# Attention fed into two mixture layers on one core: pv of the first token half one slot later, the second pair of head groups one slot later, and the q, k, v and p loads issued on SP

## The chip, the core and the metric

The kernel runs on one core of a Trainium2 chip. It is measured in device microseconds for one execution of the whole program. The engines named below are PE (TensorE: matmuls, with PEld for its weight loads), ACT (ScalarE), DVE (VectorE), POOL (GpSimd) and SP (SyncE, which here only issues DMAs). Each engine runs its own instructions in the order in which the program wrote them, and waits on semaphores for the others.

## What is computed

Cut to what matters, with 4 batches, 8 heads, 576 tokens of 64 values, 32 packed queries per head, and random float32 inputs:

```python
def sm_attn(qq, kk, vv):
    s = scale * np.matmul(qq, kk.transpose(0, 1, 3, 2))
    a = softmax(s)                     # max taken off, sum plus 1e-9
    return np.matmul(a, vv)
p_packed = sm_attn(p, k, v)            # 32 rows per head
out = sm_attn(q, p_packed, p_packed)   # 576 rows per head
x = out laid out as (2304, 512)
for e in range(4):                     # first mixture, weights by domain_probs
    y += prob[:, e:e+1] * (relu(x @ w1[e]) @ w2[e])
logits = y @ phi                       # second mixture: 8 experts, 4 slots each
d, c = softmax over tokens, softmax over slots
slot_out = expert MLP (m1, m2) of d.T @ y
result = c @ slot_out                  # (2304, 512)
```

## The kernel before, in words

A head part (about 70 us) loads weights, folds w2 and phi into one matrix, and computes the attention of batch 0. Then the main loop (`for sl in range(nslot + 1)`, L878) runs 128 slots: 32 per batch. A slot computes 2 x 6 matmuls of the first mixture (`mm1`, L477, "step M") for one expert and one block of 128 hidden features, for the batch whose attention is ready. Every fourth slot (0, 4, 8, ... of a batch) it first folds the next weights with the packed attention values (`make_g`, L447, "step G": 16 matmuls into two PSUM buffers, then two ACT casts L458 and two DVE subtractions L459, the second of which reads PSUM last) and adds logits (L504, "step L"). Beside it the attention of the next batch is computed piecewise by two generators, one for heads 0 to 3 (called g0 here) and one for heads 4 to 7 (g1). Each is resumed once per slot, in step A, and runs to its next `yield`. Within a slot the steps are written in the order F, G, L, M, S, A, P: F is the flip of the slot before (DVE L487, POOL L488), S the softmax of the batch before, P pours hidden activations of the batch before into sums (`pool_slots`, L648, in slots 4, 5 and 6 of a batch, for the batches after the first; its DVE reads are L666 to L672).

So the order on each engine is fixed by the slot in which a piece is written. In this text slot 20 is the 21st slot of a batch, G20 the step G in it, M20 its twelve matmuls and M20_1 the second six of these.

g0 starts in slot 0, g1 in slot OFF1, which is 9. A generator of a later batch does, slot by slot from its start: flip of p and of the first half of k (DVE L309, L292); flip of the second half of k and the scores `sa` (PE L301); `sa` again; maximum; exponential; scaling and transpose into `et` (DVE L332, L334); four ACT copies of the first token half of `et` into `etm` (L340); pv of the first half (36 small matmuls, L350); four copies of the second half into the same `etm`; pv of the second half with an ACT copy of the result to `gl` (L361); then the second attention with q (scores `sb`, exponential L394, and so on) until ACT casts the attention result into `a2` (L413) and POOL subtracts (L414), nine slots after the second pv.

Two resources matter below. `etm` is one buffer in the main loop, so the copies of the second half wait for pv of the first. And M, G, pv and the scores take their PSUM buffers from one ring of four (`mm_ps`), in turn; while a pv sum stands, its buffer is skipped and the others turn through three:

```python
def mm_ps(name, keep=None):
    i = (turns["mm"] + 1) % 4
    while i in kept.values():
        i = (i + 1) % 4
```

The loads of the next heads are queued as each buffer comes free (`feed`): the first half of k for the next group after pv of the first half, the second half of k after pv of the second, q after the flips of k, v after the flips of q. They are issued at the start of the slot behind (`run_due`), before by POOL. The 1 MB loads of w1 (L169) and, towards the end, the stream of the second mixture's weights (L749) are issued by SP.

Of the kernel before, what the change touches and what calls it, by code (L numbers as in the profile page):

```python
# [18 lines left out]
def tile_packed_attention_moe_softmoe(  # L19
# [15 lines left out]
    pe, act, dve, pool, sp = nc.tensor, nc.scalar, nc.vector, nc.gpsimd, nc.sync  # L35
# [20 lines left out]
    PLACE = ((0, 1, 2, 3), (4, 1, 2, 3)) * 2  # L56
    PIECES = ((0, 6), (6, 12), (12, 18))
    ENDS = ((0, 4), (4, 8), (8, 12), (12, 16), (16, 18))
    OFF1 = 9
    HEAD = "000101001011w1001w0011w10w0w1100w10w0101w1w1Gwww10w1G10w"  # L60
    LOADS = "PKkvaqVbQcXd1Wn2W3"
    WARM = 16
# [33 lines left out]
# [4 lines that stand above are left out]
        turns["mm"] = i  # L100
        if keep is not None:
            kept[keep] = i
        return ps_mm[i].tile([128, 512], F32, tag="mm", name=name)
# [25 lines left out]
    def a_tile(tag, name, bufs=1):  # L129
        return att_pool.tile([128, S], F32, tag=tag, name=name, bufs=bufs)  # L130
# [2 lines left out]

    def load_p(b, g, eng=None):
        t = att_pool.tile([128, D], F32, tag="p", name=f"p{b}{g}", bufs=2)
        (eng or pool).dma_start(t, p[b, 4 * g : 4 * g + 4].rearrange("h m d -> (h m) d"))
        qkv_t["p", b, g] = t

    def load_half(src, nm, b, g, hf, t=None, eng=None):
        if t is None:  # L140
            t = a_tile("qkv", f"{nm}{b}{g}{hf}", 4)
        t = t.rearrange("p (x d) -> p x d", d=D)
        (eng or pool).dma_start(
            t,
            src[b, 4 * g : 4 * g + 4].rearrange("h (t x) d -> (h t) x d", x=NBLK)[
                :, HB * hf : HB * hf + HB, :
            ],
        )
        qkv_t[nm, b, g, hf] = t
# [132 lines left out]
    def attention(b, g, feeds, ptb, pkb, etb, tmp, gp):  # L282
# [3 lines left out]
        def feed(key):  # L286
            if key in feeds:
                due.append(feeds[key])
# [48 lines left out]
        for hf in range(2):  # L337
            for h in range(4):
                r = slice(32 * h, 32 * h + 32)
                act.copy(  # L340
                    etb[hf % len(etb)][r, h % 2, :, 32 * (h // 2) : 32 * (h // 2) + 32],
                    et[r, HB * hf : HB * hf + HB, :],
                )
            yield
            vn = qkv_t.pop(("v", b, g, hf))
            if pv is None:
                pv = mm_ps(f"pv{bg}", bg)
            for x in range(HB):
                for par in range(2):
                    pe.matmul(  # L350
                        pv[64 * par : 64 * par + 64, :64],
                        vn[:, x, :],
                        etb[hf % len(etb)][:, par, x, :],
                        start=(hf == 0 and x == 0),
                        stop=(hf == 1 and x == HB - 1),
                        tile_position=(0, 64 * par),
                    )
            feed(f"k{hf}")
            if hf == 0:
                yield  # L360
# [59 lines left out]
    def start_attention(b, g):  # L420
        feeds = {}
        nb, ng = (b, 1) if g == 0 else (b + 1, 0)

        def later(src, nm, hf, bb, gg):
            return lambda: load_half(src, nm, bb, gg, hf)

        for hf in range(2):
            feeds[f"q{hf}"] = later(q, "q", hf, b, g)
            if nb < NB:
                feeds[f"k{hf}"] = later(k, "k", hf, nb, ng)  # L430
                feeds[f"v{hf}"] = later(v, "v", hf, nb, ng)
        if nb < NB:
            f = feeds["k0"]
            feeds["k0"] = lambda: (load_p(nb, ng), f())
        return attention(b, g, feeds, pt, pkt[:, g], [etm], att_tmp, pool)
# [335 lines left out]
    with tc.manual_schedule():  # L771
# [5 lines left out]
        def load_pair(src, nm, b, g, ts=None):  # L777
            for hf in range(2):
                load_half(src, nm, b, g, hf, ts and ts[hf], eng=sp)

        def load_next():
            load_pair(k, "k", 1, 0)
            load_p(1, 0, sp)
            load_pair(v, "v", 1, 0)

        loads = {
            "P": lambda: (load_p(0, 0, sp), load_p(0, 1, sp)),
            "K": lambda: load_pair(k, "k", 0, 0),
            "k": lambda: load_pair(k, "k", 0, 1, [hd0[:, 0], hd0[:, 1]]),
# [40 lines left out]
        def head_tmp(tag, name):  # L830
            if tag == "kt":
                return ht_pool.tile([128, S], F32, tag="ht", name=name)
            return spare[tag]

        gens = {
            "0": attention(0, 0, {}, pt, pkt[:, 0], [etm, et_x[0]], att_tmp, dve),
            "1": attention(
                0, 1, {}, pp1, pkt[:, 1], [et1, et_x[1]], head_tmp,
                pool if GP1 == "pool" else dve,
# [38 lines left out]
        for sl in range(nslot + 1):  # L878
# [3 lines left out]
            b, i = divmod(n, NU)  # L882
# [6 lines left out]
            if run and b + 1 < NB:  # L889
                if sl % 32 == 0:  # L890
                    att_gens.append(start_attention(b + 1, 0))
                if sl % 32 == OFF1:
                    att_gens.append(start_attention(b + 1, 1))
            def step_attention():
                for gen in list(att_gens):
                    if next(gen, "end") == "end":
                        att_gens.remove(gen)
                        if b + 2 == NB and not att_gens and sl % 32 > OFF1:
                            att.close()
# [94 lines left out]
        for i in range(2):  # L994
# [9 lines left out]
            for k, t in enumerate((ps, ps2)):  # L1004
                t = t.rearrange("p (j l r q) -> p r j l q", j=2, l=2, r=2)
# [127 lines left out]
        for so, (d0, dw) in zip(sos, PARTS):  # L1133
            project(1, CHUNK // dw, dw, [(so, 0, dw)])
            h = slice(d0, d0 + dw)
# [9 lines left out]
            for x0 in range(0, NBLK, nt):  # L1145
                ob = out_tile()
                for x in range(x0, x0 + nt, nb):
                    m = min(nb, x0 + nt - x)
# [41 lines left out]
```

## Time and profile before

| | |
|---|---|
| median of 3 runs | 534.63 us (533.45 to 535.47) |
| the profiled execution | 533.26 us, of which 531.5 us are the span of the core |
| PE busy | 492.4 us, 93% of the span |
| DVE, ACT, POOL busy | 55%, 44%, 47% |
| granted TensorE clock, mean | 0.984 of full speed |

The span has three stretches. The head goes to about 70 us. The main loop runs from there to about 428 us with PE nearly without a gap. After it the last sums are poured, and from about 450 us to the end the weights of the second mixture stream in with the DMA engines full. Times in the rows below are in us from the start of the span. In a row of the timeline the first number is the start, the second the duration (of all the instructions merged in the row), and the brackets tell how long the engine had stood idle before it and what ended that.

### The profile page before, as it was taken

What the parts mean: (1) busy time and instruction counts of PE and PEld (TensorE: products, weight loads), DVE (VectorE), ACT (ScalarE), POOL (GpSimd) and SP (SyncE); (2) the same over time, 40 slices, a digit from 0 to 9 for tenths busy, and PEclk for the clock granted to TensorE, in tenths of its full rate; (3) what the DMA queues carried; (4) which work ended last, traced back from release to release, by engine and by line L of the source; (5) the groups of instructions that cost most, each with busy time, mean ns of one, the idle gap of its engine ahead of it and who ended that gap; (6) DMA issues with size and microseconds to landing.
All of it is one profiled execution on the core that took longest, in us unless ns stands there. A gap on an engine that the chain in (4) does not pass through costs nothing.

```text
span 531.5 us, 12898 instructions
## 1 busy us (share of the span) xinstructions
PE 492.4 (93%) x5404; PEld 347.1 (65%) x5404; DVE 293.1 (55%) x539; ACT 235.6 (44%) x539; POOL 247.9 (47%) x310
## 2 busy tenths in 40 slices
PE   7897999999999999999998999999999987998883
PEld 5775787777865777787557778775778864224232
DVE  6265555756667666568775655676554544311031
ACT  3857555565552447465324564651345421111031
POOL 8512446597652467975326566852446531200000
PEclk9999999999999999999999999999999998998997
DMA  8999145343430353443204424351368459999998
GB/s 280 367 373 312 47 151 190 113 151 102 158 126 1 116 182 105 151 155 115 90 2 149 152 93 141 121 209 71 120 224 332 159 192 367 409 408 408 374 326 288
DMA packets 66713, 104.06 MB, mean 196 GB/s; under 512 B 4368, under 2 KB 50192, under 8 KB 66656
## 3 DMA queue, kind: packets, MB, share of 16 engines
q1 hardware_dynamic: 62640, 93.10, 49.6%
q0 software_dynamic: 3232, 9.75, 6.2%
q8 instruction: 42, 0.69, 0.6%
q10 hardware_dynamic: 784, 0.39, 0.3%
q14 instruction: 15, 0.12, 0.1%
HBM read 98.52 MB, written 4.72 MB: 194 GB/s over the span
## 4 chain that ended last, share of the span: by engine, by line
PE 65%; DMA 13%; ACT 8%; DVE 8%; issue 3%; POOL 3%; SPq 0%; POOLq 0%; DVEq 0%; ACTq 0%
PE h L477 32%; PE sl L648 7%; DMA ck<-in_moe_w_dram 7%; PE lg L504 6%; PE g L447 5%; DMA hn<-in_moe_w_dram 3%; ACT etm L340 3%; PE sa L301 3%; PE pv L350 3%; PE sb L301 3%; DMA k<-in_k_dram 2%; PE o L1151 1%; PE w2t L255 1%; POOL hn L488 1%; PE pw L241 1%
## 5 line engine op out<-in xcount | busy, mean ns | idle before, releaser
L477 PE MATMUL h<-a,g 128*128 128x288 f32 x1536 | 226.1, 302 | 2.5 <-POOL a L414 1.6
L477 PEld LDWEIGHTS h<-a,g 128*128 128x128 f32 x1536 | 208.0, 188 | 28.3 <-issue 22.3
L488 POOL TENSOR_TENSOR hn<-hn,dp_sb 128x576 f32<-128x576 f32 x128 | 151.4, 1188 | 123.2 <-DVE hn L487 118.9
L481 ACT ACTIVATE ht<-h 128x288 f32<-128x288 f32 x256 | 103.6, 411 | 149.3 <-PE h L477 149.0
L487 DVE STREAM_TRANSPOSE hn<-ht 128x576 f32<-128x576 f32 x128 | 96.6, 761 | 55.0 <-ACT ht L481 54.9
L459 DVE TENSOR_TENSOR g<-g,g 128x512 fp32r<-128x512 f32 x64 | 41.2, 685 | 26.6 <-ACT g L458 26.6
L648 PE MATMUL sl<-hn,dpt 32*32 32x512 f32 x1152 | 48.2, 597 | 1.5 <-DVE dpt L607 1.2
L458 ACT CAST g<-g 128x512 fp32r<-128x512 f32 x64 | 34.3, 588 | 21.1 <-PE g L447 21.0
L504 PE MATMUL lg<-ht,wphi 128*32 128x288 f32 x512 | 37.8, 412 | 0.0
L447 PE MATMUL g<-w,gl 64*32 64x512 f32 x512 | 35.7, 601 | 0.2 <-DVE tacc L666 0.2
L648 PEld LDWEIGHTS sl<-hn,dpt 32*32 32x32 f32 x1152 | 21.0, 103 | 21.4 <-issue 11.0
L504 PEld LDWEIGHTS lg<-ht,wphi 128*32 128x32 f32 x512 | 13.5, 109 | 32.7 <-issue 25.5
L350 PE MATMUL pv<-etm,v 128*64 128x64 f32 x468 | 19.0, 225 | 6.6 <-ACT etm L340 3.5
L414 POOL TENSOR_TENSOR a<-a,a 64x576 fp32r<-64x576 f32 x14 | 19.9, 1424 | 9.6 <-ACT a L413 8.9
L350 PEld LDWEIGHTS pv<-etm,v 128*64 128x64 f32 x468 | 16.2, 138 | 10.7 <-ACT etm L340 5.7
L340 ACT COPY etm<-et 32x288 f32<-32x288 f32 x52 | 22.3, 428 | 1.7 <-DVE et L334 0.5
L382 DVE STREAM_TRANSPOSE nat<-sb 128x288 f32<-128x288 f32 x14 | 6.8, 483 | 25.5 <-PE sb L301 25.5
L1120 PE MATMUL so<-hn,tacc 128*32 128x384 f32 (+1 forms) x104 | 18.2, 492 | 2.6 <-DMA hn<-in_moe_w_dram 2.6
L666 DVE TENSOR_TENSOR tacc<-sl,tacc 128x512 f32<-128x512 f32 (+2 forms) x32 | 15.3, 546 | 9.4 <-PE sl L648 9.4
L260 ACT COPY hn<-w2t 128x512 f32<-128x512 f32 x32 | 17.1, 588 | 6.0 <-PE w2t L255 6.0
L255 PE MATMUL w2t<-ident,hn 128*128 128x128 f32 x128 | 17.4, 279 | 2.2 <-ACT hn L260 2.2
L301 PE MATMUL sa<-k,pt 128*128 128x288 f32 x56 | 16.7, 425 | 1.9 <-DVE k L292 1.4
(179 smaller groups left out, 484.8 us busy)
## 6 DMA issues: line engine op xcount, KB each, us to landing
w<-in_moe_w_dram SPq DMA_DIRECT2D x32, 1024.0 KB, 5.4
hn<-in_moe_w_dram SPq DMA_DIRECT2D x42, 512.0 KB, 9.5
ck<-in_moe_w_dram SPq DMA_DIRECT2D x42, 512.0 KB, 9.1
hn<-in_moe_w_dram SPq DMA_DIRECT2D x14, 384.0 KB, 8.5
q<-in_q_dram POOLq DMA_DIRECT2D x12, 288.0 KB, 3.3
k<-in_k_dram POOLq DMA_DIRECT2D x10, 288.0 KB, 3.3
v<-in_v_dram POOLq DMA_DIRECT2D x10, 288.0 KB, 3.3
out_dram<-ob SPq DMA_DIRECT2D x7, 384.0 KB, 5.2
```

What stands on the lines that cost most here:

```text
L301: pe.matmul(ps[:, :HS], lhs[:, j, :], t[:, :, j, :], start=(j == 0), stop=(j == 1))
L340: act.copy(etb[hf % len(etb)][r, h % 2, :, 32 * (h // 2) : 32 * (h // 2) + 32], et[r, HB * hf : HB * hf + HB, :],)
L350: pe.matmul(pv[64 * par : 64 * par + 64, :64], vn[:, x, :], etb[hf % len(etb)][:, par, x, :], start=(hf == 0 and x == 0), stop=(hf == 1 an ...
L447: pe.matmul(pss[g][32 * ((c + 2 * g) % 4) : 32 * ((c + 2 * g) % 4) + 32, :], gl[b % 2][r, c, :], t[r, c], start=True, stop=True, tile_posi ...
L458: act.copy(hi, pss[g])
L459: dve.tensor_tensor(out=lo, in0=pss[g], in1=hi.bitcast(F32), op=ALU.subtract)
L477: pe.matmul(ps[:, :HS], gg[:, l, g, e % 2, fs], r[:, ts], start=(g == 0 and t == 0), stop=(g == 1 and t == 2),)
L481: act.activation(out=ht[:, ts], in_=ps[:, :HS], func=AF.Relu)
L487: dve.transpose(out=own, in_=unturned.pop((n, kf, e)).rearrange("p (x t) -> p x t", t=32))
L488: pool.tensor_tensor(out=own, in0=own, in1=dp_sb[:, n // NU, :, e].unsqueeze(2).to_broadcast([128, NBLK, 32]), op=ALU.mult,)
L504: pe.matmul(lg_t[b, pr][32 * c : 32 * c + 32, :HS], wphi[:, 2 * i + kf, 32 * e : 32 * e + 32], ht_t[n, kf, e][:, HS * hf : HS * hf + HS], ...
L648: pe.matmul(pss[f][c : c + 32, :], dpt[r, x, :], hn[r, p0 : p0 + NU, x, 2 * ep : 2 * ep + 2].rearrange("p n e k f -> p n (e k f)"), start= ...
```

## The change

Three edits. The first load line of each helper takes SP instead of POOL as its default engine: this concerns the 37 loads of q, k, v and p in the main loop, since those of the head name SP already. `OFF1` goes from 9 to 10, so g1 starts a slot later. And for batches after the first an extra `yield` stands between the four copies of the first half into `etm` and pv of that half. All that follows in a generator comes a slot later; with the later start, g1 is two slots later from its first pv on. (The printed line numbers of the changed kernel are two higher from L345 on.)

```diff
-    OFF1 = 9
+    OFF1 = 10
...
     def load_p(b, g, eng=None):
...
-        (eng or pool).dma_start(t, p[b, 4 * g : 4 * g + 4].rearrange("h m d -> (h m) d"))
+        (eng or sp).dma_start(t, p[b, 4 * g : 4 * g + 4].rearrange("h m d -> (h m) d"))
...
     def load_half(src, nm, b, g, hf, t=None, eng=None):
...
-        (eng or pool).dma_start(
+        (eng or sp).dma_start(
...
             yield
+            if b and not hf:
+                yield
             vn = qkv_t.pop(("v", b, g, hf))
```

Three places show how this moves the instructions. In the names, h2_0_2_1 is the second token half (last digit) of the first mixture for block 2 and expert 2 (first and third digit); g3_0 the folded weights of block 3; a2_10 and a2_11 the attention result of the next batch; pv3, et3 belong to g1 of batch 1, pv4 to g0 of batch 2. A wait in brackets names the engine waited for.

ACT around slots 18 to 20 of the first batch of the loop, before:

```order
L413 CAST a2_10_1469<-a22_1444 64x576 [waits DVE_49]
L413 CAST a2_11_1470<-a22_1444 64x576
L361 COPY gl1_114<-pv3_1400 128x64 [waits PE_49]
L481 ACTIVATE ht2_1_1_1498<-h2_1_1_0_1499 128x288 [waits PE_49]
L481 ACTIVATE ht2_1_1_1498<-h2_1_1_1_1507 128x288 [waits PE_49]
L458 CAST g3_0_1529<-g3_0_0_1530 128x512 [waits PE_49]
L458 CAST g3_0_1529<-g3_0_1_1531 128x512 [waits PE_49]
```

The same place after the change:

```order
L483 ACTIVATE ht2_1_1_1467<-h2_1_1_0_1468 128x288 [waits PE_49,Activation_49]
L483 ACTIVATE ht2_1_1_1467<-h2_1_1_1_1476 128x288 [waits PE_49]
L415 CAST a2_10_1484<-a22_1440 64x576 [waits DVE_49]
L415 CAST a2_11_1485<-a22_1440 64x576
L340 COPY etm_117<-et3_1347 32x9x32 [waits Activation_49] x4
L460 CAST g3_0_1496<-g3_0_0_1497 128x512 [waits PE_49]
L460 CAST g3_0_1496<-g3_0_1_1498 128x512 [waits PE_49]
```

The two casts into `a2` and the four copies of the second half now stand between the last relu of slot 19 and the casts of G20; before, the relus of slot 19 stood there alone.

PE in slot 20 of the same batch, before:

```order
L477 MATMUL h2_0_2_0_1553<-a2_00_660,g2_1_1356 128x288 x3
L477 MATMUL h2_0_2_0_1553<-a2_01_661,g2_1_1356 128x288 x3
L477 MATMUL h2_0_2_1_1561<-a2_00_660,g2_1_1356 128x288 x3
L477 MATMUL h2_0_2_1_1561<-a2_01_661,g2_1_1356 128x288 x3
L477 MATMUL h2_0_3_0_1578<-a2_00_660,g2_1_1356 128x288 [waits DVE_49]
```

And after:

```order
L479 MATMUL h2_0_2_0_1520<-a2_00_660,g2_1_1351 128x288 x3
L479 MATMUL h2_0_2_0_1520<-a2_01_661,g2_1_1351 128x288 x3
L479 MATMUL h2_0_2_1_1528<-a2_00_660,g2_1_1351 128x288 [waits DVE_49]
L479 MATMUL h2_0_2_1_1528<-a2_00_660,g2_1_1351 128x288 x2
L479 MATMUL h2_0_2_1_1528<-a2_01_661,g2_1_1351 128x288 x3
L352 MATMUL pv3_1442<-etm_117,v111_1268 64x64 [waits DMAHW3_49,Activation_49]
```

M20_1 had no wait and now has one on DVE; pv of the second half, which stood in slot 18, follows it.

PE at slots 7 and 8 of the second batch of the loop, before:

```order
L477 MATMUL h4_1_3_1_2286<-a2_11_1470,g4_1_1859 128x288 x3
L350 MATMUL pv4_2294<-etm_117,v200_1525 64x64 [waits DMASW4_49,DVE_49,Activation_49]
L350 MATMUL pv4_2294<-etm_117,v200_1525 64x64 [waits Activation_49]
L350 MATMUL pv4_2294<-etm_117,v200_1525 64x64 x16
L447 MATMUL g5_1_0_2320<-w1_5_1_1910,gl1_114 32x512 [waits DMAHW7_49,DVE_49]
L447 MATMUL g5_1_1_2321<-w1_5_1_1910,gl1_114 32x512 [waits Activation_49]
```

And after:

```order
L479 MATMUL h4_1_3_0_2278<-a2_11_1485,g4_1_1859 128x288 x3
L479 MATMUL h4_1_3_1_2286<-a2_10_1484,g4_1_1859 128x288 [waits Activation_49]
L479 MATMUL h4_1_3_1_2286<-a2_10_1484,g4_1_1859 128x288 x2
L479 MATMUL h4_1_3_1_2286<-a2_11_1485,g4_1_1859 128x288 x3
L449 MATMUL g5_1_0_2297<-w1_5_1_1910,gl1_114 32x512 [waits DMAHW5_49,DVE_49]
L449 MATMUL g5_1_1_2298<-w1_5_1_1910,gl1_114 32x512 [waits DVE_49]
```

With pv gone from between them, G8 follows M7 at once, and both of its buffers now wait for DVE, not one.

## Rows read from the trace of the kernel before

**Rows 1.** Windows: start:end, length, busy (x count) by engine, PEclk, DMA share, GB/s

```profile
70.00:95.00 25.00, 23.81 (x245) 18.84 (x245) 15.07 (x25) 13.04 (x32) 14.46 (x23) 1.00 0.49 159
...
376.00:428.00 52.00, 52.00 (x475) 42.22 (x476) 27.43 (x38) 25.09 (x58) 29.22 (x25) 1.00 0.59 213
...
434.00:444.00 10.00, 9.34 (x288) 5.79 (x256) 1.41 (x4) 0.00 (x0) 0.46 (x2) 1.00 0.63 218
...
464.00:474.00 10.00, 10.00 (x73) 2.84 (x72) 2.06 (x4) 1.59 (x4) 0.00 (x0) 1.00 1.03 409
```

**Rows 2.** Timeline of PE, first batch of the loop, slots 4 to 10

```profile
66.40 6.63 PE L477 MATMUL h<-a,g 128*128 128x288 f32 x48
73.40 1.72 PE L350 MATMUL pv<-etm,v 128*64 128x64 f32 x36 [0.37 <-ACT etm L340]
...
82.91 1.86 PE L477 MATMUL h<-a,g 128*128 128x288 f32 x12 [0.30 <-ACT gl L361]
```

**Rows 3.** Timeline, second and third batch, slot 7: PE and DVE

```profile
172.13 1.85 PE L477 MATMUL h<-a,g 128*128 128x288 f32 x12
172.19 2.48 DVE L666 TENSOR_TENSOR tacc<-sl,tacc 128x512 f32<-128x512 f32 x4 [2.72 <-PE sl L648]
...
174.18 1.27 PE L350 MATMUL pv<-etm,v 128*64 128x64 f32 x36 [0.20 <-issue]
...
274.32 1.86 PE L477 MATMUL h<-a,g 128*128 128x288 f32 x12
274.38 2.74 DVE L666 TENSOR_TENSOR tacc<-sl,tacc 128x384 f32<-128x384 f32 x8 [2.80 <-PE sl L648]
...
276.72 1.27 PE L350 MATMUL pv<-etm,v 128*64 128x64 f32 x36 [0.54 <-ACT ht L481]
```

**Rows 4.** Timeline, first batch, slots 15 to 18: PE, ACT and DVE

```profile
98.84 1.09 PE L447 MATMUL g<-w,gl 64*32 64x512 f32 x16
...
99.54 0.68 ACT L394 ACTIVATE nat<-nat 128x576 f32<-128x576 f32 x1 [0.18 <-POOL nat L390]
...
100.13 1.78 ACT L340 COPY etm<-et 32x288 f32<-32x288 f32 x4
...
100.97 1.86 PE L477 MATMUL h<-a,g 128*128 128x288 f32 x12
...
101.93 1.07 ACT L458 CAST g<-g 128x512 fp32r<-128x512 f32 x2
102.55 1.29 DVE L459 TENSOR_TENSOR g<-g,g 128x512 fp32r<-128x512 f32 x2 [1.93 <-ACT g L458]
...
103.29 1.27 PE L350 MATMUL pv<-etm,v 128*64 128x64 f32 x36 [0.46 <-DVE g L459]
```

**Rows 5.** Timeline, first batch, slot 18: PE, ACT and POOL

```profile
108.22 1.71 PE L350 MATMUL pv<-etm,v 128*64 128x64 f32 x36 [0.27 <-ACT etm L340]
...
109.38 1.37 ACT L413 CAST a<-a 64x576 fp32r<-64x576 f32 x2
...
110.13 2.92 POOL L414 TENSOR_TENSOR a<-a,a 64x576 fp32r<-64x576 f32 x2 [0.43 <-ACT a L413]
```

**Rows 6.** Timeline: loads of k with what waits, third batch; scores of the second

```profile
188.15 1.21 PE L301 MATMUL sa<-k,pt 128*128 128x288 f32 x4 [0.48 <-ACT ht L481]
...
279.13 14.85 SPq L169 DMA_DIRECT2D w<-in_moe_w_dram  x2
...
279.59 0.54 POOL L143 DMA_DIRECT2D k<-in_k_dram  x1
...
285.85 0.78 DVE L292 STREAM_TRANSPOSE k<-k 128x576 f32<-128x576 f32 x1 [1.82 <-DMA k<-in_k_dram]
...
286.93 0.58 POOL L143 DMA_DIRECT2D k<-in_k_dram  x1 [2.50 <-DVE k L292]
...
290.34 0.78 DVE L292 STREAM_TRANSPOSE k<-k 128x576 f32<-128x576 f32 x1 [2.39 <-DMA k<-in_k_dram]
...
291.26 1.21 PE L301 MATMUL sa<-k,pt 128*128 128x288 f32 x4 [1.07 <-DVE k L292]
```

## The prediction, made before the changed kernel was run

> **What bounds the kernel now.** I read the windows first. In the last 52 us of the main loop PE is busy throughout, and in a stretch with attention beside it, 70 to 95 us, it is idle for 25.00 - 23.81 = 1.2 us [rows 1]. So the loop is bound by PE, and an edit can win there only PE's short waits, some 1 to 2 us in 25. The stretch behind it is bound differently: the DMA share is 0.63 while the last sums are poured (434 to 444 us) and 1.03 from 464 us [rows 1]. The stream gets much of its space when those sums are done, so it starts when PE lets it: what the loop gains or loses, the end gains or loses too, and the tail gives nothing back. I therefore went through the timeline of PE, wait by wait, for the three batches that carry attention, and then followed the same waits through the new order.
>
> The waits before, in us, are these. Slot 7 of the first batch: pv of g0's first half waits 0.37 for the copies into `etm`, and its 36 matmuls then take 1.72 where 1.27 do elsewhere, since the second matmul waits for the last copy: 0.82 in all [rows 2, 3]. In the second and third batch the sums of the batch before delay slot 6, the copies are long done, and the same pv waits only 0.20 and 0.54 [rows 3]. pv of g1's first half waits 0.46 for DVE's subtraction of G16, since its PSUM buffer is the one that G16 filled [rows 4]; the other two batches show the same. pv of the second half waits 0.27 and runs 1.71 - 1.27 = 0.44 longer [rows 5]; so do all six such pv's. The M behind g0's second pv waits 0.30 for the copy to `gl`, in each batch [rows 2]. And the scores of g1 wait 0.48 and 1.07 for the flip of k in the second and third batch, because the load came late [rows 6].
>
> **The change part by part.**
>
> pv of g0's first half, slot 7 to 8. The copies now have a whole slot, G8 and L8 before pv: the waits of 0.82, 0.20 and 0.54 go, a gain of 1.56. pv then takes the buffer of G8, but G and L take 100.97 - 98.84 = 2.13 and M8 another 1.86 [rows 4], and ACT is free for G8's casts at once, so DVE's subtraction, 1.36 after the cast begins (103.29 - 101.93), is past by then.
>
> What comes up in its place: pv stood between M7 and G8 and took one of the two buffers that the last pour of slot 6 had filled. Without it G8 comes at the end of M7 and needs both, and DVE has read both only when its `tacc` row ends. In the second batch that is 172.19 + 2.48 = 174.67 against an end of M7 at 172.13 + 1.85 = 173.98, in the third 277.12 against 276.18 [rows 3]. That costs 0.69 and 0.94, 1.63 together; in the first batch nothing is poured. From below it can cost nothing if the first buffer's matmuls run ahead of the second's, but they alternate; I take 1.63 whole.
>
> pv of g0's second half keeps its setting, copies one slot ahead and no G between: its 0.71 stays.
>
> pv of g1's first half, slot 16 to 18. The wait on G16 goes. The copies come after M16, and before them stands the exponential of g0: 0.59 until the copies begin and 1.78 for them [rows 4]. With ACT about 0.5 behind the end of M16 they are done 2.9 behind it; M17 and M18 take 3.3 at least (6.63 for four [rows 2]). pv's buffer is that of M17's first half, whose relu comes just after the copies. I put the wait left at 0.1 and the gain at 3 x 0.36 = 1.08; the bounds are 0 and 3 x 0.46.
>
> pv of g1's second half, slot 18 to 20. It now has G20 and L20 before it, more than the copies need: 3 x 0.71 = 2.13 gained.
>
> The price of that is in M20, and it is the largest term. While the pv sum of g1 stands (slots 18 to 20) three buffers turn: M19 takes two, G20 the third and one of these again, M20 the next and then the first one of G20. So M20_1 waits until DVE has subtracted G20's first half, and DVE waits for ACT's cast. On ACT, however, g0's two casts into `a2` (1.37 [rows 5]) and g1's four copies now stand ahead of that cast, all written in slot 19. Counted from the start of G20 as the rows show it for G16: the last relu ends at 99.36 - 98.84 = 0.52 (the exponential starts at 99.54 after 0.18 idle); the `a2` casts take it to 1.9; the copies, 100.13 to the cast at 101.93, to 3.7; cast to release 1.36, to 5.07 [rows 4, 5]. PE is at M20_1 after 2.13 and half of 1.86, 3.06. The wait is 2.0, three times 6.0. Its uncertainty is that of ACT's lag, some 0.3 each way: 5.1 to 6.9. Before, the same three buffers turned at G8 (g0's sum stood there), but ACT held only relus, and no wait came of it. What is late next: nothing on PE, since pv of the second half is then behind its copies anyway.
>
> The wait on `gl`. After the turn of the buffers the M behind g0's second pv no longer takes the freed buffer, but M21 behind g1's does: 0.30 moves, net 0.
>
> g1 two slots later at its end. The casts into `a2` move from slot 27 to 29; M32 needs POOL's two subtractions. From the end of M29: 0.5 until ACT is free, half of 1.37, then 2.92 on POOL: 4.1, or 5.3 with one POOL multiply in the way [rows 5]; M30, M31, G32 and L32 take 3.3 + 2.1 = 5.4. Hidden, with little cover in the worse case: I take 0 and keep 0.6 a batch as the upper bound.
>
> The loads on SP. POOL loses 37 issues of 0.54 to 0.58 [rows 6]. PE waits for POOL nowhere in the rows of the loop: 0. What counts is the pair of k loads behind each other: the second half's load waits for the flip of the first half (idle 2.50 in the third batch), and before both stood among POOL's multiplies [rows 6]. Now only SP's queue is ahead. The scores of the second half also move behind G12 and L12, so the waits of 0.48 and 1.07 go whatever the loads do within 2 us: 1.55 gained. Behind a waiting load on SP stand the w1 loads. They are used eight slots after their buffer comes free, over 15 us, and the longest such wait here is 2.50: 0.
>
> The sum: gains 1.56 + 1.08 + 2.13 + 1.55 = 6.32; losses 6.0 + 1.63 = 7.63; **1.3 us slower**. The profiled execution, 533.26 us with 531.5 of span, would become 534.6. It ran 1.4 below the median of 534.63; on the median I forecast **535.9 us**.
>
> **The rivals.**
>
> *M20_1 does not wait.* If ACT had the cast of G20 done before the copies, or the buffer were free, all gains stand and only the 1.63 is lost: 6.32 - 1.63 = 4.7 faster, 529.9 us. For it speaks that the same turn of three buffers costs nothing at G8 now; against it that the new order has a wait on DVE there, and four copies and two casts ahead of the cast. It decides by its size: at a wait of 1.56 a batch (4.69 in three) the change breaks even, below 0.67 it is faster by more than 2.67.
>
> *The loads of k come late on SP*, which ends slower. A load of k issued 0.46 after a w1 load took from 279.59 to 285.85, 6.3 us, until its flip; the next one, alone, 286.93 to 290.34, 3.4 [rows 6]. From the end of g0's first pv, PE has four M (7.0), the second pv with its wait (1.9), one `sa` (1.0) and G12 with L12 (2.1) before the second scores: 12.0. The two loads have to be followed by two flips, one flip of step F (0.78 each) and half of 1.29 for the buffer, 3.0. So the two together may take 9.0; at 3.4 twice there is slack of 2.2, at 6.3 and 3.4 they are 0.7 late, 2.0 in three batches: 537.9 us. Only one w1 load is issued between G8 and G12, about 4 us ahead of the first k load now, which speaks against it. [...]
>
> *The loads buy nothing*: the scores of g1 wait as before in spite of their later place, 1.55 is not gained, 537.5 us. Their 2.13 of added cover speaks against it.
>
> **How the numbers follow.** Forecast as summed 0.70, its own range 533.9 to 537.9 from the bounds of M20_1 (0.9 each way), the moved `a2` (up to 1.8), the pv's of g1 and the run's spread of 1.0; M20_1 without a wait 0.12; late loads 0.13; loads that buy nothing 0.05. A measurement of this kernel tells about 0.5%, 2.67 us, from no change, so faster means below 531.96 and slower above 537.30. Faster is the first rival and 0.01 of the forecast, 0.13; slower are the other two and 0.05 of the forecast's upper end, 0.23; the same 0.64. The range from 533.0 to 539.0 leaves out the first rival and the far end of the late loads.
>
> **What would show it.** In the profile after: pv of first halves at 1.27 without waits; a wait of 2 us of an M (h) on DVE's subtraction (g) three times, at slot 20, with two `a2` casts and four copies right before the cast on ACT; G8 waiting 0.7 and 0.9 on `tacc` in the second and third batch; the pv's of g1 without waits, those of g0's second half as before; no `sa` waiting. Wrong would make it: no wait at M20_1, a pair of k loads that takes over 9 us, or a tail that does not shift with the loop.

## The result, and the profile after

The changed kernel took 540.5 us (median; 538.92 to 542.64) against 534.76 us (533.45 to 535.47) before: ratio 1.0125, 95% interval 1.0101 to 1.0148, so 5.7 us or 1.2% slower. The forecast was 535.9 us with a range to 539.0: the sign of its sum was right, its size was not. The profiled execution took 540.03 us, with 538.2 us of span.

Where the time went is seen first by cutting the span. I call loop the stretch from the start of M3 of the first batch to the first `lt` of the last batch (a matmul behind that batch's softmax, written after the last M). In the timeline of PE these are, before:

```profile
62.38 1.96 PE L477 MATMUL h<-a,g 128*128 128x288 f32 x12
...
428.62 0.76 PE L556 MATMUL lt<-ls,fold 64*128 64x288 f32 x4
```

and after:

```profile
62.35 1.96 PE L479 MATMUL h<-a,g 128*128 128x288 f32 x12
...
433.98 0.76 PE L558 MATMUL lt<-ls,fold 64*128 64x288 f32 x4
```

The loop went from 366.24 to 371.63, 5.39 us more, and nothing was added ahead of it. Behind it the span is another 1.3 us longer, but in the thirteen profiles of this study that tail lies anywhere from 102.9 to 104.2 us with no relation to what was changed. The head varies too (M3 starts at about 62.4 or about 64.0 us). So kernels are compared below by the length of the loop, beside the measured medians.

The list of PE's waits after (total us, times, longest) names the large term:

```profile
PE h L479 <- DVE g L461: 5.8, 3, 1.9
```

This line is M20_1, once in each batch. The timeline of PE shows it, and the pv's of the first batch, with the rows that answer to [rows 2, 4, 5]:

```profile
76.96 1.27 PE L352 MATMUL pv<-etm,v 128*64 128x64 f32 x36
81.87 1.71 PE L352 MATMUL pv<-etm,v 128*64 128x64 f32 x36 [0.27 <-ACT etm L340]
...
105.02 1.27 PE L352 MATMUL pv<-etm,v 128*64 128x64 f32 x36
...
113.13 1.06 PE L479 MATMUL h<-a,g 128*128 128x288 f32 x6 [1.93 <-DVE g L461]
114.12 2.06 PE L352 MATMUL pv<-etm,v 128*64 128x64 f32 x36
116.48 5.61 PE L479 MATMUL h<-a,g 128*128 128x288 f32 x36 [0.30 <-ACT gl L363]
...
217.03 1.07 PE L479 MATMUL h<-a,g 128*128 128x288 f32 x6 [1.93 <-DVE g L461]
218.03 1.27 PE L352 MATMUL pv<-etm,v 128*64 128x64 f32 x36
219.61 5.04 PE L479 MATMUL h<-a,g 128*128 128x288 f32 x36 [0.31 <-ACT gl L363]
...
321.03 1.06 PE L479 MATMUL h<-a,g 128*128 128x288 f32 x6 [1.94 <-DVE g L461]
322.02 1.80 PE L352 MATMUL pv<-etm,v 128*64 128x64 f32 x36
324.13 5.85 PE L479 MATMUL h<-a,g 128*128 128x288 f32 x36 [0.30 <-ACT gl L363]
```

The first pv's of g0 and g1 run in 1.27 without a wait, as forecast. M20_1 waits 1.93, 1.93 and 1.94. And now the rows that were not forecast: behind the wait, pv and the 36 matmuls take 1.27 and 5.04 in the second batch, but 2.06 and 5.61 in the first and 1.80 and 5.85 in the third. The windows say why. Columns: PE, weight loads, DVE, ACT, POOL busy, then the granted clock of TensorE, the DMA share and GB/s:

```profile
113.00:114.00 1.00, 0.87 (x6) 0.83 (x6) 0.67 (x2) 0.15 (x1) 0.46 (x1) 1.00 0.43 145
114.00:115.00 1.00, 1.00 (x21) 0.88 (x21) 0.33 (x1) 0.41 (x1) 0.00 (x0) 0.66 0.00 0
115.00:116.00 1.00, 1.00 (x22) 0.98 (x20) 1.00 (x2) 0.00 (x0) 0.41 (x1) 0.50 0.00 0
...
118.00:119.00 1.00, 1.00 (x9) 1.00 (x8) 0.00 (x0) 0.47 (x2) 0.55 (x3) 1.00 0.94 301
...
218.00:219.00 1.00, 1.00 (x33) 0.97 (x34) 0.42 (x1) 0.41 (x1) 0.00 (x0) 1.00 0.00 0
```

After the idle stretch the granted clock fell to 0.50 and was back at 1.00 from 118 us on; in the second batch, behind an equal wait, it stayed at 1.00. The lower clock costs 0.79 + 0.57 = 1.36 in the first batch and 0.53 + 0.81 = 1.34 in the third.

What keeps M20_1 waiting stands on ACT and DVE in the timeline of slots 19 and 20, as the prediction had worked it out:

```profile
108.56 1.37 ACT L415 CAST a<-a 64x576 fp32r<-64x576 f32 x2
109.95 1.79 ACT L340 COPY etm<-et 32x288 f32<-32x288 f32 x4
111.76 1.07 ACT L460 CAST g<-g 128x512 fp32r<-128x512 f32 x2
...
112.38 1.29 DVE L461 TENSOR_TENSOR g<-g,g 128x512 fp32r<-128x512 f32 x2 [3.04 <-ACT g L460]
```

Two more losses show in the timeline. G8, in the second and third batch, where [rows 3] had pv:

```profile
176.34 1.68 PE L449 MATMUL g<-w,gl 64*32 64x512 f32 x16 [0.17 <-DVE tacc L668]
...
280.26 1.79 PE L449 MATMUL g<-w,gl 64*32 64x512 f32 x16 [0.42 <-PE h L479]
```

A G takes 1.09 [rows 4], so this is 0.17 + 0.59 = 0.76 and 0.42 + 0.70 = 1.12. (The second bracket names PE itself, but M7 had ended by then; DVE's adds into `tacc` run from 278.08 to 280.82 there, into G8.) And the scores of g0 at slots 32 and 33 (the first slots of the next batch), which had no wait before:

```profile
142.39 3.49 POOL L490 TENSOR_TENSOR hn<-hn,dp_sb 128x576 f32<-128x576 f32 x3
...
145.21 1.29 DVE L544 TENSOR_TENSOR ls<-ls,dpe 128x576 f32<-128x576 f32 x1
...
147.43 0.78 DVE L292 STREAM_TRANSPOSE k<-k 128x576 f32<-128x576 f32 x1
...
148.36 1.21 PE L301 MATMUL sa<-k,pt 128*128 128x288 f32 x4 [0.27 <-DVE k L292]
...
151.41 1.21 PE L301 MATMUL sa<-k,pt 128*128 128x288 f32 x4 [0.25 <-DVE k L292]
```

DVE's product into `ls` (step S of slot 32, the softmax of the batch before) takes 1.29, before it took 0.76:

```profile
141.09 1.19 POOL L488 TENSOR_TENSOR hn<-hn,dp_sb 128x576 f32<-128x576 f32 x1 [0.32 <-DVE hn L487]
...
143.56 0.76 DVE L542 TENSOR_TENSOR ls<-ls,dpe 128x576 f32<-128x576 f32 x1
```

Before, POOL was done at 142.28 when the product began at 143.56. After, POOL's subtractions of `a2` come two slots later, the multiplies behind them run to 145.88, and the product that begins at 145.21 has one beside it. The flips of p and k come later by as much, and `sa` waits: 0.27 + 0.25 here, 0.27 + 0.26 in the next batch.

| term, us in the loop | forecast | after |
|---|---|---|
| first pv of g0 | -1.56 | -1.56 |
| first pv of g1 | -1.08 | -1.39 |
| second pv of g1 | -2.13 | -2.13 |
| `sa` of g1 | -1.55 | -1.55 |
| G8 on `tacc` | +1.63 | +1.88 |
| M20_1's wait | +6.0 | +5.80 |
| lower clock behind that wait | not seen | +2.70 |
| `sa` of slots 32 and 33 | 0 | +1.05 |
| sum | +1.3 | +4.80, of 5.39 measured |

### The profile page after: what moved, and what is told of

Its sections match the earlier page's. It is cut to its first block, busy times and chain, and to the rows that moved or that the text cites. A ratio compares the mean times of both kernels' runs of the same rounds, so it can differ in the third digit from the quotient of the medians.

```text
span 538.2 us, 12901 instructions
## 1 busy us (share of the span) xinstructions
PE 495.6 (92%) x5404; PEld 348.4 (65%) x5404; DVE 297.0 (55%) x539; ACT 234.8 (44%) x539; POOL 228.4 (42%) x273
## 4 chain that ended last, share of the span: by engine, by line
PE 68%; DVE 11%; DMA 9%; ACT 7%; issue 2%; POOL 0%; SPq 0%; DVEq 0%; ACTq 0%; POOLq 0%
PE h L479 34%; PE sl L650 7%; PE g L449 6%; PE lg L506 6%; DMA ck<-in_moe_w_dram 5%; DMA hn<-in_moe_w_dram 3%; PE pv L352 3%; PE sb L301 3%; ACT etm L340 2%; PE sa L301 2%; PE si L1029 1%; PE o L1153 1%; DVE tacc L670 1%; PE w2t L255 1%; PE pw L241 1%
## 5 line engine op out<-in xcount | busy, mean ns | idle before, releaser
L489 DVE STREAM_TRANSPOSE hn<-ht 128x576 f32<-128x576 f32 x128 | 97.7, 765 | 68.4 <-ACT ht L483 68.1
L449 PE MATMUL g<-w,gl 64*32 64x512 f32 x512 | 37.0, 601 | 0.8 <-PE h L479 0.4
L255 PEld LDWEIGHTS w2t<-ident,hn 128*128 128x128 f32 x128 | 13.9, 141 | 6.9 <-ACT hn L260 4.8
```

Source lines behind the costliest of these rows:

```text
L255: pe.transpose(ps[:, 128 * dc : 128 * dc + 128], w2_row(ft, e)[:, 128 * dc : 128 * dc + 128], ident,)
L449: pe.matmul(pss[g][32 * ((c + 2 * g) % 4) : 32 * ((c + 2 * g) % 4) + 32, :], gl[b % 2][r, c, :], t[r, c], start=True, stop=True, tile_posi ...
L489: dve.transpose(out=own, in_=unturned.pop((n, kf, e)).rearrange("p (x t) -> p x t", t=32))
```

## Experiments

Theory: the order of ACT's work around slot 20 costs the time, by M20_1's wait and by the clock behind it, with POOL's later subtractions as a smaller part. Rivals: the loads on SP cost it; or any later start of g1 does, whatever stands on ACT. All ratios are to the kernel before on the same chip; the length of the loop is from the profiled execution.

| kernel | median, us | ratio, 95% interval | loop, us |
|---|---|---|---|
| before | 533.5 to 534.8 | 1 | 366.24 |
| after | 540.5 | 1.0125 (1.0101 to 1.0148) | 371.63 |
| after, loads on POOL | 540.61 | 1.0132 (1.0095 to 1.0170) | 373.23 |
| before, loads on SP | 532.33 | 0.9983 (0.9966 to 0.9999) | 364.24 |
| before, OFF1 = 10 | 538.46 | 1.0093 (1.0061 to 1.0126) | 369.84 |
| after, no yield in g1 | 533.86 | 1.0010 (0.9995 to 1.0025) | 365.65 |
| after, casts of g0 one slot later | 536.08 | 1.0042 (1.0028 to 1.0056) | 367.29 |
| after, wait of M20_1 filled | 537.49 | 1.0071 (1.0054 to 1.0088) | 369.04 |
| after, OFF1 = 11 | 534.08 | 0.9996 (0.9982 to 1.0010) | 364.97 |
| after, casts of g1 one slot earlier | 540.03 | 1.0106 (1.0077 to 1.0136) | 372.30 |
| OFF1 = 11, casts of both earlier | 537.70 | 1.0070 (1.0048 to 1.0091) | 369.38 |
| OFF1 = 11, g1 two yields less | 533.18 | 0.9984 (0.9969 to 0.9998) | 364.36 |
| OFF1 = 11, g1 one yield less | 532.61 | 0.9981 (0.9966 to 0.9995) | 364.63 |

**The loads, taken back and alone.** The first undoes one part of the change, the second does that part alone.

In the changed kernel, at both helpers (`load_p` and `load_half`):

```
-        (eng or sp).dma_start(
+        (eng or pool).dma_start(
```

And in the kernel before, at the same two lines:

```
-        (eng or pool).dma_start(
+        (eng or sp).dma_start(
```

> The changed kernel with the loads of q, k, v and p issued by POOL again; the extra yield and OFF1 = 10 stay. Theory (the order around slot 20 costs the time: M20_1's wait of 1.93 three times, the lower granted clock behind it in two batches, the sums at slots 32 and 33): all of it stays, ratio to the kernel before 1.010 to 1.013, about 540.5 us; M20_1 waits 1.9 three times. Rival (the loads on SP cost it, in the loop or by the queue of the tail): ratio 1.000 to 1.003, about 535.5 us.

> The kernel before with the loads issued by SP, nothing else. Theory: no wait of PE goes by more than the 0.48 and 1.07 us of sa, ratio 0.997 to 1.001, 533 to 535 us. Rival (the loads on SP cost the time): ratio 1.008 to 1.012, about 540 us.

With the loads back on POOL the whole loss stays (1.0132), M20_1 waiting 1.94 three times and the clock falling behind it in all three batches (mean 0.87, 0.88 and 0.89 in 112 to 125, 216 to 230 and 320 to 336 us); alone, the loads on SP make the kernel a little faster (0.9983, the interval just below 1). So they do not cost the time. In the kernel with the loads alone, the two `sa` of g1 that waited 0.48 and 1.07 [rows 6] wait no more, in the timeline of PE:

```profile
187.56 1.13 PE L301 MATMUL sa<-k,pt 128*128 128x288 f32 x4
...
289.38 1.13 PE L301 MATMUL sa<-k,pt 128*128 128x288 f32 x4
```

That was the gain of 1.55 in the forecast, and the loads bring it by themselves, without the later slot; the loop is 2.0 shorter.

**A later g1 alone, and without its yield.** No run has the yield alone with OFF1 = 9: g1's second half of k would then be flipped in slot 10, and its load, queued behind pv of g0's second half in that slot, is issued only at the start of the next.

```
-    OFF1 = 9
+    OFF1 = 10
```

> The kernel before with OFF1 = 10, nothing else: g1 one slot later, its pv's in slots 17 and 19, so that no G lies in the stretch in which its sum stands. Theory: M20_1 does not wait and the clock stays up; the waits of g1's first pv (0.46 each) and of sa (0.48, 1.07) go: 532 to 533 us, ratio 0.995 to 0.998. Rival (a later g1 costs by itself, through its a2 casts and POOL's subtraction running into the softmax of slot 32): a ratio above 1.003, 536.5 us or more.

```
-            if b and not hf:
+            if b and not hf and g == 0:
                 yield
```

> The changed kernel with the extra yield for g0 only; g1 then has its pv's in slots 17 and 19. Theory: M20_1's wait and the lower clock behind it go (5.8 + 2.6), the waits of g1's second pv (0.71 each) come back (2.1): 6.3 below the changed kernel, about 534 us, ratio 0.996 to 1.001. Rival (the loss lies in g0's later pv, G8 waiting on tacc, and in the loads): ratio 1.007 or more, 538 us.

The second came out as the theory said (1.0010, the upper end of its range): without g1's extra yield the loss is gone. The first did not: OFF1 = 10 alone costs 0.9%, the rival's number. But its rows show ACT again, at another place. The casts of g0 come in slot 18 there, and so do the four copies of g1's second half; in the timeline of ACT and PE:

```profile
108.45 1.37 ACT L413 CAST a<-a 64x576 fp32r<-64x576 f32 x2
109.84 1.79 ACT L340 COPY etm<-et 32x288 f32<-32x288 f32 x4
...
111.23 2.25 PE L350 MATMUL pv<-etm,v 128*64 128x64 f32 x36 [1.66 <-ACT etm L340]
```

pv of the second half waits 1.66 in place of 0.27, in all three batches, and once the clock fell behind it (0.50 from 113 to 115 us; pv 2.25, where 1.71 is usual). I had counted only the waits for PSUM buffers and not what the copies themselves stand behind. With the yield in g0, its casts move to slot 19, and this is what the second kernel of this pair has. So the later start as such is not the cause; which of ACT's pieces share a slot is.

**The casts behind those of G20.**

```
+        if b and g == 0:
+            yield
         for r in range(2):
             rows = slice(64 * ((r + g) % 2), 64 * ((r + g) % 2) + 64)
```

> The changed kernel with one more yield in g0 (batches after the first) ahead of its two casts into a2, so that they are written in slot 20 behind the casts of G20 and no longer ahead of them. Theory (the collision on ACT of two a2 casts and four copies ahead of the cast of G20): M20_1's wait falls from 1.93 by the 1.37 of the casts to 0.5 to 0.6, the granted clock stays at 1.00 behind it; the loop loses 4.1 and 2.6 us of what the change cost, ratio to the kernel before 0.998 to 1.002. Rival (the wait is that of three PSUM buffers alone, whatever stands on ACT): M20_1 waits 1.9 as before, ratio 1.010 or more.

PE's timeline, first batch; the other two read the same:

```profile
111.99 1.07 PE L481 MATMUL h<-a,g 128*128 128x288 f32 x6 [0.55 <-DVE g L463]
...
115.19 5.05 PE L481 MATMUL h<-a,g 128*128 128x288 f32 x36 [0.93 <-ACT gl L363]
```

The wait fell by 1.38, the length of the casts, to 0.55, and the clock held in all three batches (pv 1.27, the 36 matmuls 5.05): the theory's mechanism. The ratio, 1.0042, missed its 1.002, since the casts now stand ahead of the copy to `gl`: that wait grew from 0.30 to 0.93, 1.9 in three batches. What was moved on ACT came late for someone else.

**The wait filled with work.** This kernel adds matmuls whose result nobody reads.

```
+            if hf and n % NU == 2 and kf == 0 and e == 2 and b + 1 < NB:
+                fp = tr_ps(f"fill{n}")
+                for _ in range(6):
+                    pe.transpose(fp[:, :128], ident, ident)
             ps = mm_ps(f"h{n}_{kf}_{e}_{hf}")
```

> The changed kernel with six transposes of the identity into a free PSUM buffer between M20_0 and M20_1 in the three batches that carry attention: some 1.64 us of TensorE work (6 x 0.273) that nobody reads, in the place of the wait. Theory (the idle time lowers the granted clock, and what stands behind it runs longer): M20_1 begins when it did, the clock behind it stays at 1.00, pv takes 1.27 and the 36 matmuls behind it 5.0 in each batch: about 2.6 us below the changed kernel, ratio to the kernel before 1.006 to 1.009. Rival (the longer times behind the wait have another cause than the idle time): they stay, ratio 1.011 to 1.015.

```profile
106.60 1.27 PE L352 MATMUL pv<-etm,v 128*64 128x64 f32 x36
...
112.61 0.82 PE L477 MATMUL fill<-ident 128*128 128x128 f32 x6
114.71 1.06 PE L483 MATMUL h<-a,g 128*128 128x288 f32 x6 [1.28 <-DVE g L461]
115.70 1.27 PE L352 MATMUL pv<-etm,v 128*64 128x64 f32 x36
117.28 5.04 PE L483 MATMUL h<-a,g 128*128 128x288 f32 x36 [0.31 <-ACT gl L363]
```

The six transposes took 0.82, half of what I had reckoned. M20_1 starts 8.11 after the first pv of g1, as without them (113.13 - 105.02), so the wait is the same; but pv takes 1.27 and the 36 matmuls 5.04, in all three batches. The loop is 2.59 shorter than that of the changed kernel, against 2.70 summed from its rows, and the intervals of the two ratios don't meet. The clock term is shown: useless work in the gap made the kernel faster.

**OFF1 = 11.** The copies of the second half then come in slot 20, behind the casts of G20.

```
-    OFF1 = 10
+    OFF1 = 11
```

> The changed kernel with OFF1 = 11: the sum of g1's pv then stands in slots 19 to 21, and the four copies of the second half come behind the casts of G20 instead of ahead of them; the two a2 casts of g0 stay ahead. Theory: M20_1 waits 1.93 - 1.79 = 0.1 to 0.3, no lower clock; the second pv of g1 waits for its copies again (0.71 each, 2.1): 535 us, ratio 0.999 to 1.004; g1's casts into a2 come another slot later, and the waits at slots 32 and 33 or at M32 grow by up to 1 us a batch. Rival (every later start of g1 costs more): ratio 1.012 or more.

M20_1 waits no more, pv of the second half waits 0.28 as before, and the loss is gone (0.9996):

```profile
113.54 1.71 PE L352 MATMUL pv<-etm,v 128*64 128x64 f32 x36 [0.28 <-ACT etm L340]
```

g1 is later than in the changed kernel here, and the time is 1.3% shorter by the two ratios: this settles the rival by which a later start costs. g0's two casts still stand ahead of the casts of G20 here, so neither the casts alone nor the copies alone (a wait of 0.55 above) make the whole wait of 1.93; both together do. It has a price at slot 32, where the product into `ls` takes 1.72 and `sa` waits 0.56 and 0.26.

**The casts of g1 one slot earlier.**

```
         dve.transpose(out=a2.rearrange("p (x t) -> p x t", t=32), in_=nat)
-        yield
+        if not (b and g):
+            yield
```

> The changed kernel without the yield between the flip of a2 and the casts into a2 in g1 (batches after the first), so that casts and subtractions come one slot earlier. Theory (POOL's subtractions, two slots later, push its multiplies beside DVE's product of the softmax in slot 32): that product takes 0.76 again, not 1.29, and the waits of 0.27 and 0.25 of sa in slots 32 and 33 go; 1.1 us below the changed kernel, ratio 1.009 to 1.012. Rival (those waits come of the later k loads): they stay.

POOL's multiplies are done earlier against the product, which is back to 0.84, and `sa` at slots 32 and 33 waits no more:

```profile
142.57 4.63 POOL L491 TENSOR_TENSOR hn<-hn,dp_sb 128x576 f32<-128x576 f32 x4
...
146.98 0.84 DVE L545 TENSOR_TENSOR ls<-ls,dpe 128x576 f32<-128x576 f32 x1
```

That part of the theory holds in the rows. The ratio, 1.0106, lies in the expected range, but its interval takes in the changed kernel's, so the time alone would not tell; in this execution the clock fell behind M20_1 in all three batches (mean 0.87 to 0.89 in the stretches given above), and its loop is the longer for it.

**Both moves together, in three forms.** All have OFF1 = 11. The first drops the yield above for g0 as well, the second drops it for g1 and also the one behind the second exponential, the third for g1 alone. At the flip of `a2`, in the first:

```
-        yield
+        if not b:
+            yield
```

At the flip and behind the exponential (`L396`) in the second, and at the flip alone in the third:

```
-        yield
+        if not (b and g):
+            yield
```

> The changed kernel with OFF1 = 11 and, for batches after the first, without the yield between the flip of a2 and the casts into a2: the a2 casts of g0 come in slot 18, the copies of g1's second half in slot 20 behind the casts of G20, and g1's a2 casts in slot 29. Theory (two collisions, that of a2 casts, copies and G20's cast on ACT, and that of POOL's multiplies with DVE's product in slot 32): both are gone, M20_1 does not wait, the product takes 0.8, no sa waits in slots 32 and 33; against the same kernel with OFF1 = 11 alone that is 0.56 + 0.26 in two batches, 1.6 us less: 532 to 533 us, ratio 0.995 to 0.998. Rival (the loop is bound otherwise, and what is taken from one wait comes up in the next): ratio 0.999 to 1.002.

> The changed kernel with OFF1 = 11 and, in g1 of batches after the first, without two yields: the one behind the second exponential and the one between the flip of a2 and the casts into a2. g1's casts then come in slot 28, as in a kernel whose g1 is one slot late; g0 keeps all its yields. Theory (POOL's subtractions in slot 30 push its multiplies beside DVE's product in slot 32): the product falls from 1.72 to some 0.85 and sa in slots 32 and 33 does not wait, 1.6 us below OFF1 = 11 alone: 532 to 533 us, ratio 0.995 to 0.998. Rival (a cast on ACT or a sum on DVE that now waits in its slot for another engine holds the relus or the subtractions behind it, as the casts of g0 in slot 18 did): an M or G of slots 27 to 29 waits 0.3 or more in each batch, ratio 0.999 to 1.004.

> The changed kernel with OFF1 = 11 and, in g1 of batches after the first alone, without the yield between the flip of a2 and the casts into a2, so that these come in slot 29; g0 keeps its yields, and its casts stay in slot 19. Theory (in the version that moved both, the 1.5 us a batch were lost by g0's casts in slot 18, which waited for DVE and held a relu of M19): G20 does not wait, the product in slot 32 takes 1.29, 0.6 us below OFF1 = 11 alone at most, ratio 0.997 to 1.001. Rival (the loss lay with g1's casts or elsewhere): ratio 1.005 or more.

The first was a miss, 1.0070. It shows the same fault a third time. Its timeline of ACT and PE in slots 18 to 20:

```profile
109.09 1.36 ACT L416 CAST a<-a 64x576 fp32r<-64x576 f32 x2 [1.19 <-DVE a L406]
...
109.35 1.04 PE L450 MATMUL g<-w,gl 64*32 64x512 f32 x2
110.94 1.09 PE L450 MATMUL g<-w,gl 64*32 64x512 f32 x14 [0.55 <-ACT ht L484]
```

ACT waits 1.19 for DVE's flip of `a2`, and the relus behind the casts come late; while a pv sum stands, G20 needs their PSUM buffer, and its first two matmuls and its wait end 1.59 after its start. Per batch that is the 1.5 us by which its loop exceeds that of OFF1 = 11. I had also counted wrongly: with OFF1 = 11 a cast of g1 one slot earlier comes in slot 29, where the changed kernel has it, so slot 32 could not gain.

The third form leaves g0 alone, and G20 does not wait: the loss of the first lay with g0's casts. The second form's ratio, 0.9984, lies just above the range given for it, the third's within. In the second and third the product into `ls` takes 1.35 and 1.62, more than I expected, and `sa` waits 0.33 and 0.25, and 0.56 and 0.25. Where a cast stands in the text is not what decides; when POOL gets through its queue is. These two and the kernel with the loads alone are the fastest (0.9981 to 0.9984), about 1 us below the kernel before and 7 to 8 below the changed one; they can't be told from each other.

## Why the prediction was wrong

What bounds the loop, and that the end passes on what the loop loses, held: 5.39 in the loop, 5.7 in the medians.

The gains were right to 0.3 us. The waits of three kinds of pv and of g1's `sa` went as the steps said, those of g0's second halves stayed. That `sa` would gain from its later slot was one of two reasons; the loads on SP do it alone.

M20_1, the largest term, was right in place, cause and size: 2.0 forecast, 1.93 measured, with casts, copies and G20's cast in the order worked out. The rival "M20_1 does not wait" is refuted. G8 was right in place and cause, 1.88 for the 1.63 that I took whole. The wait on `gl` moved to M21 at no cost.

The step that failed is the sentence behind that term, "What is late next: nothing on PE". A wait was priced at its length. Behind it the granted clock fell in two batches of three, and that is 2.70 more, which the filled wait took away. The profile before had the sign of it, behind the loop. There `tt0a` begins at 446.69 after 3.36 us of idle time of PE, and `hidt` at 483.60 after 1.73, the stretch nearest in length to the 2.0 us forecast. The rows of `hidt` in the timeline and of both in the windows:

```profile
483.60 1.66 PE L1084 MATMUL hidt<-ident,wphi 128*128 128x128 f32 x8 [1.73 <-DVE wphi L1080]
...
447.00:448.00 1.00, 1.00 (x6) 1.00 (x5) 0.00 (x1) 0.17 (x1) 0.00 (x0) 0.50 1.07 434
...
484.00:485.00 1.00, 1.00 (x7) 0.86 (x5) 0.55 (x2) 0.00 (x0) 0.00 (x0) 0.51 1.08 430
```

The granted clock, the third figure from the end, is at or near 0.50 behind both. PE's longest wait in [rows 2 to 6] is 1.07, and the clock held there (1.00 from 291 to 294 us), so the price of 2 us had to be bounded from these rows, and I did not.

A second step was mis-sized: the moved `a2` was taken at 0, with 0.6 a batch kept as a bound. It cost 0.52 and 0.53 in two batches, 1.05, but not on the way I checked. I followed POOL's subtraction to M32, which needs it, and found cover; the cost came from POOL's multiplies behind it, which run beside DVE's product (1.29 in place of 0.76) and delay the flip of k. I had counted what waits for the moved step, and not what the step pushes ahead of it on its own engine.

The loads on SP at 0 were right in cost, and the rival by which they come late is refuted: after, the loads of k took 2.9 us at the median from issue to landing. What became of a load behind a w1 load on SP shows in the loads of p, for which PE does not wait. After, the five of the loop were issued on SP 0.43 behind a w1 load and landed 4.8 to 5.4 us later, 0.2 to 0.5 after that load; before, the two that POOL issued at the same moment as a w1 load took 4.0 and 4.1 and landed 1.6 and 2.1 ahead of it. The loads of k were issued farther from a w1 load and took 2.6 to 3.6 in the loop: after, the nearest was issued 4.0 us behind a w1 load that landed 1.0 later, and with the loads alone, in the third batch, 1.1 us ahead of one.

With the two missing terms, 2.70 + 1.05, the sum of 1.3 becomes 5.1 of 5.39. The rows in the table sum to 4.80, and what they lack shows at the first `sb` of g1 (its scores with q). Two slots later, it stands ahead of G24 and no longer ahead of an M. In the second batch, before:

```profile
218.14 1.13 PE L301 MATMUL sb<-q,pkt 128*128 128x288 f32 x4
218.89 1.97 PE L477 MATMUL h<-a,g 128*128 128x288 f32 x12
```

and after:

```profile
224.49 1.13 PE L301 MATMUL sb<-q,pkt 128*128 128x288 f32 x4
225.56 1.09 PE L449 MATMUL g<-w,gl 64*32 64x512 f32 x16
```

What follows `sb` starts 1.07 behind its start, before 0.75; it is so in all three batches, some 0.95 together, a term that the prediction did not have. No run tested it alone. With it the rows sum to 5.75, a little over the 5.39; the two waits of g1's `sa` are worth more than the 1.55 of their brackets, since with the loads alone the loop is 2.0 shorter.

The range ended at 539.0 because it had no price for the clock; the chance of slower, 0.23, was too small for the same reason. The cost of the moved `a2` lay inside the bound kept for it.

## What to carry to other kernels

Before a piece of work is moved on an engine, list what it will share its slot with on that engine and who waits for the last of them; here two casts of 1.37 us cost PE 1.4 to 1.5 us a batch in three different places, by what they kept waiting (M20_1 0.55 or 1.93, pv 0.27 or 1.66, G20 none or 1.5). Price a new idle stretch of TensorE by its length and by the clock behind it, from the nearest stretch of the profile where TensorE waited that long. A step that is moved also moves what is queued behind it, and that can come to run beside another engine's instruction that is longer for it: DVE's product here, 1.29 us for 0.76.

## What the hardware showed

**The clock behind a wait.** Behind the 1.93 us waits of M20_1 the granted clock fell (to 0.50 in the changed kernel) in eight of nine cases (two of three in the changed kernel, three of three with the loads on POOL and with g1's casts earlier), behind the 1.66 us waits of pv in one of three, and in none of three where 1.28 us of idle time were left behind the filler, nor behind waits of 0.55 and 0.93. A wait that long is not needed, though: with the loads on POOL, without g1's yield and with g1's casts earlier, the mean granted clock over the head (0 to 70 us) was 0.98, and no wait of PE there was longer than 1.4 us. Nor is one of 1.5 us enough: before and after, the mean over the head was 1.00, with waits of 1.51 and 1.59 in it. By their rows, seven of the nine falls behind the waits of M20_1 and pv cost some 1.3 to 1.5 us of PE's time each. That equal waits in one execution ended differently was not expected, and what decides it is open.

**DVE's product beside POOL.** The product into `ls` was the longer, 0.76 to 1.72 us, the more of POOL's multiplies ran beside it. From the starts and ends in the timelines (second batch of the loop):

| kernel | POOL beside it, us | product, us |
|---|---|---|
| before | 0 | 0.76 |
| casts of g1 earlier | 0.22 | 0.84 |
| after | 0.67 | 1.29 |
| OFF1 = 11, two yields less | 0.72 | 1.35 |
| OFF1 = 11, one yield less | 1.00 | 1.62 |
| OFF1 = 11 | 1.10 | 1.72 |

The third row is read from the two rows shown of the changed kernel: POOL ends at 142.39 + 3.49 = 145.88, 0.67 after the product began at 145.21, and the product is 0.53 longer than alone. In the last four rows the excess is 0.8 to 0.9 of the overlap, while POOL's multiplies take 1.16 each, as before (4.62 for four). What makes it so is not shown.
